# A new order of the same steps, and 113 copies on the other engine, in a one-core attention and MLP kernel

## Chip, core and metric

One core of one Trainium2 chip runs the whole kernel. The metric is device time in microseconds (us); the kernel before takes 613.71 us, the median of three runs (613.70, 613.71, 615.13).

## What is computed

Attention with rotated queries and keys (batch 4, 8 heads, 576 tokens, 64 wide), then a two-layer MLP on its 2304 rows of 512, with 2048 hidden columns and a piecewise quadratic activation:

```python
q_rot, k_rot = rotate(q), rotate(k)
scores = np.matmul(q_rot, k_rot.transpose(0, 1, 3, 2)) / np.sqrt(D)
scores = scores - np.max(scores, axis=-1, keepdims=True)
attn = np.exp(scores)
attn = attn / (np.sum(attn, axis=-1, keepdims=True) + 1e-09)
x = np.matmul(attn, v).transpose(0, 2, 1, 3).reshape(B * S, H * D)
h = x @ w_in
g = np.where(h >= 1, h, np.where(h <= -1, 0.0, (h + 1) ** 2 / 4))
return g @ w_out
```

## The kernel before

**Numbers.** Products run on float16 pairs: a value is its rounded high part and the rest as low part, and a product is the sum of three matmuls (high by high, high by low, low by high). The high part is a plain scaled copy, which either ACT (line 314) or DVE (line 316) can make; the low part (line 324, or 545 in the softmax) is always DVE's. Batch 0 alone multiplies its scores in float32 (line 562), the others use pairs (line 564).

**Stages.** Weights come in eight chunks of w_in and w_out (`prep_w`, 1 MB loads at line 239). DVE joins their words in three steps (493, 495, 497), ACT makes the high part, PE subtracts it (430, 431) and ACT writes the low part (434). Queries and keys are rotated by DVE (`turn`, lines 287 to 295; the first k halves with PE's help, 305 and 306). v is squared for its scale (248), split into `vS`, and copied by DMA to the other partitions as `vM`. An item is one tile of 128 rows for one pair of heads: PE scores into `psS`, DVE takes the row maximum (534), ACT the exponential (536), DVE the reciprocal (541), then the high and low part go into `phl`, a DMA transpose (243) writes `pT`, and PE multiplies by v (612). `x_out` (623, 626) leaves the pair `xT`, the MLP's input. A step of the MLP is PE's first product into the one bank `psH` (720), ACT's copy `a` (737), the square `r` on DVE (732) or in two passes on ACT (734, 735), DVE's sum (740), the high part `g` on ACT (743) or DVE (746), the low part on DVE (748), and PE's second product (757). Finished rows are copied by ACT (770) and stored by SP.

**What sets the order.** The kernel first lists its 2180 steps in a `Plan`, each with its engine. `Plan.order` then takes them off that list by the numbers of `ORDER`: each number is the place, in what is left of the list, of the step that is written next. An engine runs its steps in the order in which they are written, one after the other; a step that waits holds all behind it on its engine. SP issues every load, store and transpose, so a transpose that waits for its `phl` holds the loads behind it. `Plan.pick` reads `ON_VECTOR`, one character for each high copy that may run on either engine (softmax, k, q, v, square, `g`; 328 in all): 1 is DVE, 0 is ACT.

```python
def pick(self, first="act", ahead=0):
    i = len(self.free)
    self.free.append(len(self.steps) + ahead)
    return ("dve" if ON_VECTOR[i] == "1" else "act") if i < len(ON_VECTOR) else first

def order(self):
    left = list(range(len(self.steps)))
    return [self.steps[left.pop(int(k))][3] for k in ORDER.split()]
```

Of the kernel before, what the change touches and what calls it, by code (L numbers as in the profile page):

```python
# [24 lines left out]
0 0 1 0 21 6 47 24 31 1 18 5 0 27 4 0 6 38 6 17 16 13 24 3 1 54 19 0 9 19 31 4 28 1 0 26 8 21 0 11 235 0 238 12  # L25
58 0 235 235 235 1 36 0 232 35 446 231 1 0 229 33 228 1 0 13 225 229 5 224 9 11 225 226 0 2 220 223 217 219 0 1
218 40 217 0 216 224 39 215 6 0 213 213 415 218 76 20 1 216 19 0 33 1 405 211 0 399 201 0 0 29 14 0 397 204 204
27 0 12 201 0 206 11 194 198 11 1 192 0 194 2 9 8 195 8 8 374 3 28 187 191 6 189 186 8 0 1 4 2 183 0 1 2 29 179 5
0 0 3 0 166 0 172 1 165 0 0 10 169 1 173 0 8 162 0 162 0 6 0 1 0 158 3 1 162 151 154 0 0 6 151 156 154 148 0 5
151 0 0 144 148 148 3 20 1 145 150 9 2 38 142 27 137 0 145 139 142 136 0 6 2 133 137 133 133 135 0 4 131 170 0  # L30
131 0 0 127 1 136 7 36 1 124 132 126 264 157 6 0 155 0 121 128 152 127 121 2 149 3 0 123 0 8 1 128 115 7 118 114
138 1 116 124 112 115 6 1 0 2 74 110 3 0 28 111 249 130 0 7 79 104 126 119 0 0 5 116 1 0 212 1 101 95 1 1 98 8 97
227 1 93 91 3 93 101 91 0 93 5 0 1 95 88 213 94 213 212 96 21 87 0 2 0 206 91 0 83 0 209 6 81 200 79 85 2 197 204
84 82 5 0 193 184 196 76 0 21 189 189 1 2 189 75 188 9 187 196 2 184 8 183 69 1 0 180 190 180 0 5 65 1 0 176 1 62
173 0 68 0 7 171 175 66 172 66 0 6 166 64 167 0 56 165 5 173 55 60 55 12 66 0 158 133 157 53 56 0 154 1 153 150
61 1 155 149 60 1 153 59 7 0 143 149 0 49 5 45 0 143 0 137 1 140 0 139 1 134 137 141 8 1 135 38 134 1 6 312 0 0 0
106 105 1 128 39 122 33 10 1 1 122 0 42 120 16 0 40 105 27 291 115 0 114 26 0 112 4 27 2 0 106 109 114 2 106 105
85 9 20 102 29 0 1 104 27 104 18 102 18 7 100 16 99 16 0 0 96 91 20 99 94 5 89 93 1 91 0 25 3 92 24 89 90 24 75
87 1 86 9 83 93 78 83 9 81 83 21 76 1 85 78 3 68 0 6 2 8 5 71 68 76 72 74 7 73 62 69 71 80 7 67 12 62 67 50 7 63
66 19 48 69 62 7 60 47 66 10 0 45 57 6 60 15 54 0 14 42 41 50 7 52 0 39 45 42 55 44 39 46 66 2 159 45 2 51 40 43  # L40
338 10 46 43 2 41 35 2 35 40 35 34 2 37 35 36 143 7 35 2 33 35 16 139 32 16 32 6 2 29 2 130 2 27 129 3 11 23 121
11 3 122 2 24 20 126 298 2 312 2 0 125 20 1 0 110 4 17 14 4 115 280 285 108 114 0 12 106 0 11 104 2 25 103 10 101
2 266 23 101 101 0 1 106 21 98 96 21 26 101 94 253 96 1 93 25 6 19 94 6 18 6 245 87 1 19 1 15 5 1 84 15 20 233 7
19 1 9 78 0 9 10 10 225 13 10 72 67 77 68 9 69 76 67 68 72 11 9 211 70 15 10 65 0 63 9 12 61 62 9 60 60 69 11 59
57 17 59 57 63 8 2 55 9 185 7 5 58 490 7 57 6 50 54 1 49 9 5 50 2 55 7 48 4 47 4 50 2 45 48 178 3 171 47 3 1 7 44
2 170 43 40 6 41 166 2 40 2 37 43 4 37 4 31 39 0 38 0 37 29 31 145 35 31 41 2 30 2 5 30 38 125 28 35 5 132 0 4 26
# [877 lines left out]
```

## Time and profile before

| | us | share of the span |
|---|---|---|
| median of three runs | 613.71 | |
| the profiled execution | 613.75 | |
| its span, first to last instruction | 612.0 | 100% |
| TensorE matmuls (PE) busy | 577.5 | 94% |
| TensorE weight loads (PEld) busy | 377.0 | 62% |
| VectorE (DVE) busy | 512.1 | 84% |
| ScalarE (ACT) busy | 414.8 | 68% |

The shares are averages over the whole span, and the engines' busy times overlap. Which engine others wait for differs from stretch to stretch, so the rows below are taken by stretch: busy time of each engine, then the gaps. In a row of an engine's timeline the bracket at the end gives the idle time ahead of the instruction and what ended it. Matmuls are pipelined, so the distance from one start to the next says more than the duration of one.

### The profile page before, as it was taken

Reading aid. Unit: us, or ns where it says so; the run is one execution under the profiler, and the core shown is the slowest. Engines: PE = TensorE matmul, PEld = TensorE weight load, DVE = VectorE, ACT = ScalarE, POOL = GpSimd, SP = SyncE. Lnnn points to the kernel's source line nnn. Section 1 sums busy time; section 2 is a strip of 40 time slices with the busy share of each in tenths; the row PEclk is TensorE's granted clock in tenths of the full one; section 3 lists DMA queues with packets and bytes.
Section 4 is the critical chain, followed back from the end, with each engine's and each line's share of the span. In section 5 each row is a group of like instructions: output and inputs, shape, how many; then the busy total and the mean of one; then the engine's idle time right before and its main releaser. Section 6 shows DMA issues by size and latency. Waiting matters only on the chain.

```text
span 612.0 us, 12593 instructions
## 1 busy us (share of the span) xinstructions
PE 577.5 (94%) x5074; PEld 377.0 (62%) x5074; DVE 512.1 (84%) x824; ACT 414.8 (68%) x844; POOL 0.7 (0%) x6
## 2 busy tenths in 40 slices
PE   4777998999999999999979999999999999999996
PEld 2434565666665767666657676666667666667673
DVE  5997998999999999999978899999878888824442
ACT  1886998999988888776867576857856474343121
POOL 0000000000000000000000000000000000000000
PEclk9868999999999999999999999999999999999999
DMA  8997999678968965897484756748544654700000
GB/s 298 329 305 173 325 307 253 173 176 148 240 159 171 241 148 94 143 149 205 82 229 94 140 107 113 136 79 140 120 78 91 95 123 91 122 19 17 2 36 17
DMA packets 182570, 91.32 MB, mean 149 GB/s; under 512 B 170608, under 2 KB 171888, under 8 KB 180464
## 3 DMA queue, kind: packets, MB, share of 16 engines
q1 hardware_dynamic: 182512, 90.52, 65.8%
q8 instruction: 39, 0.64, 0.4%
q14 instruction: 19, 0.16, 0.1%
HBM read 40.96 MB, written 4.72 MB: 75 GB/s over the span
## 4 chain that ended last, share of the span: by engine, by line
PE 55%; DVE 20%; ACT 10%; DMA 10%; issue 3%; SPq 1%; DVEq 0%; ACTq 0%
PE psH L720 20%; PE psO L757 20%; PE psV L612 6%; PE psS L564 4%; DVE phl L545 4%; DVE sca L534 4%; ACT p L536 3%; DMA pT<-phl 2%; ACT phl L314 2%; DVE r L740 2%; DVE g L748 2%; DMA dup<-in_km_dram 1%; PE psS L430 1%; PE psS L562 1%; DMA vM<-vS 1%
## 5 line engine op out<-in xcount | busy, mean ns | idle before, releaser
L720 PE MATMUL psH<-xT,w 128*128 128x256 f16 (+1 forms) x2112 | 206.8, 253 | 5.1 <-ACT a L737 5.0
L757 PE MATMUL psO<-w,g 128*128 128x512 f16 x864 | 203.3, 379 | 0.0
L720 PEld LDWEIGHTS <-w 128*128 128x128 f16 x2112 | 175.0, 98 | 38.9 <-issue 8.8
L536 ACT ACTIVATE p<-psS,sca 128x576 f32<-128x576 f32 x144 | 105.8, 737 | 49.3 <-DVE sca L534 31.0
L757 PEld LDWEIGHTS <-g 128*128 128x128 f16 x864 | 81.4, 98 | 83.8 <-issue 2.6
L545 DVE SCALAR_TENSOR_TENSOR phl<-p,sca,phl 128x576 f16<-128x576 f32 x144 | 115.9, 813 | 5.0 <-ACT phl L314 4.2
L534 DVE TENSOR_REDUCE sca<-psS 128x1 f32<-128x576 f32 x144 | 105.9, 751 | 10.0 <-PE psS L564 4.9
L314 ACT ACTIVATE phl<-p,sca 128x576 f16<-128x576 f32 x99 | 74.6, 767 | 19.1 <-DVE sca L541 10.7
L737 ACT ACTIVATE a<-psH 128x512 f32<-128x512 f32 x72 | 42.5, 590 | 62.3 <-PE psH L720 58.1
L740 DVE SCALAR_TENSOR_TENSOR r<-a,r 128x512 f32<-128x512 f32 x72 | 49.4, 687 | 19.9 <-ACT r L735 19.2
L748 DVE SCALAR_TENSOR_TENSOR g<-r,g 128x512 f16<-128x512 f32 x72 | 49.4, 686 | 7.6 <-ACT g L743 5.5
L564 PE MATMUL psS<-kT,qT 64*128 64x64 f16 (+1 forms) x576 | 44.9, 284 | 1.0 <-ACT p L536 1.0
L612 PE MATMUL psV<-pT,vS 128*64 128x320 f16 (+2 forms) x576 | 44.2, 277 | 1.0 <-DMA pT<-phl 1.0
L564 PEld LDWEIGHTS <-qT 64*128 64x128 f16 x576 | 22.5, 94 | 30.6 <-issue 13.8
L743 ACT ACTIVATE g<-r 128x512 f16<-128x512 f32 x41 | 25.6, 624 | 13.9 <-DVE r L740 7.1
L732 DVE SCALAR_TENSOR_TENSOR r<-a 128x512 f32<-128x512 f32 x28 | 19.3, 689 | 18.4 <-ACT a L737 18.0
L612 PEld LDWEIGHTS <-vS 128*64 128x64 f16 x576 | 28.0, 111 | 9.3 <-issue 5.7
L734 ACT ACTIVATE r<-a 128x512 f32<-128x512 f32 x44 | 27.4, 624 | 6.7 <-DVE g L748 6.1
L434 ACT ACTIVATE w<-psS,sca 128x341 f16<-128x341 f32 (+1 forms) x48 | 25.3, 539 | 7.8 <-PE psS L431 7.2
L612 PE MATMUL psV<-pT,vM 128*64 128x320 f16 (+2 forms) x360 | 26.0, 275 | 3.1 <-DMA vM<-vS 3.1
L735 ACT ACTIVATE r<-r 128x512 f32<-128x512 f32 x44 | 27.7, 630 | 1.4
L536 ACT ACTIVATION_READ_ACCUMULATOR p<-psS,sca 128x1 f32 x144 | 28.3, 196 | 0.0
(95 smaller groups left out, 522.9 us busy)
## 6 DMA issues: line engine op xcount, KB each, us to landing
w<-in_w_in_dram SPq DMA_DIRECT2D x7, 1024.0 KB, 6.4
w<-in_w_out_dram SPq DMA_DIRECT2D x6, 1024.0 KB, 8.0
rv<-in_vm_dram SPq DMA_DIRECT2D x8, 512.0 KB, 6.2
out_dram<-o SPq DMA_DIRECT2D x16, 256.0 KB, 2.4
rk<-in_km_dram SPq DMA_DIRECT2D x6, 576.0 KB, 5.4
dup<-in_km_dram SPq DMA_DIRECT2D x6, 576.0 KB, 4.5
rq<-in_qb_dram SPq DMA_DIRECT2D x4, 640.0 KB, 6.7
dup<-in_qb_dram SPq DMA_DIRECT2D x4, 640.0 KB, 4.0
```

The lines of the kernel that those rows point to most:

```text
L314: plan.add("act", act_cost(n), at, lambda: nc.scalar.activation(out=hi, in_=x, func=AF.Copy, scale=f), r=r, w=w)
L534: plan.add("dve", dve_cost(S, psum=True), at, lambda m=m, src=src: nc.vector.tensor_reduce(out=m, in_=src, op=ALU.max, axis=AX.X, negate=T ...
L536: plan.add("act", act_cost(S, psum=True, ptrs=2), at, lambda a=a, e=e, m=m, src=src: nc.scalar.activation(out=p32[e], in_=src, func=AF.Exp ...
L545: plan.add("dve", dve_cost(S, ptrs=1), at, lambda a=a, e=e, hi=hi, lo=lo: nc.vector.scalar_tensor_tensor(out=lo, in0=p32[e], scalar=rr[:, ...
L564: nc.tensor.matmul(out=psS[a][:, lo:hi], lhsT=qT[hf][d, l, j, c:c + 128], rhs=kT[ks][d, j, m, lo:hi], start=z == 0, stop=z == 2)
L612: nc.tensor.matmul(out=outs[a], lhsT=st, rhs=moving(a, blk), start=z == 0, stop=z == len(seq) - 1)
L720: nc.tensor.matmul(out=psH[:, n * i:n * i + n], lhsT=wi[ft // 2][:, wl, kk, 128 * (ft % 2):128 * (ft % 2) + 128], rhs=xfn(xl, kk), start=z ...
L735: nc.scalar.activation(out=r_s, in_=r_s, func=AF.Square, scale=-1.0, bias=1.0)
L737: plan.add("act", act_cost(512, psum=True, ptrs=0), at, lambda one=one: nc.scalar.activation(out=a, in_=psH, func=AF.Relu, scale=2.0 ** -7 ...
L740: plan.add("dve", dve_cost(512), at, lambda one=one: nc.vector.scalar_tensor_tensor(out=r, in0=a, scalar=one, in1=r, op0=ALU.max, op1=ALU. ...
L748: plan.add("dve", dve_cost(512), at, lambda g=g, one=one: nc.vector.scalar_tensor_tensor(out=g[:, 1], in0=r, scalar=-one, in1=g[:, 0], op0 ...
L757: nc.tensor.matmul(out=psO[pos[tt]], lhsT=g[:, gl, n * i + 128 * tt:n * i + 128 * tt + 128], rhs=wo[ft // 2][:, wl, ft % 2, :], start=ft = ...
```

## The change

Only the two tables differ: the numbers of `ORDER`, and `ON_VECTOR`. The steps, what each computes and what each needs are the same. In `ON_VECTOR` 113 of the 328 characters differ: 50 copies go from ACT to DVE and 63 from DVE to ACT. Of the softmax's 576-wide copies 21 go to DVE and 28 to ACT, of the squares 9 and 14, of the `g` copies 16 and 18, of those of k, q and v 4 and 3. A copy of either table's first lines:

```diff
 ORDER = """
-0 0 1 0 21 6 47 24 31 1 18 5 0 27 4 0 6 38 6 17 16 13 24 3 1 54 19 0 9 19 31 4 28 1 0 26 8 21 0 11 235 0 238 12
+1 30 0 0 0 26 73 6 6 11 0 9 33 22 15 0 19 0 13 1 0 59 78 20 58 37 1 0 0 16 53 0 19 1 0 23 48 243 0 47 16 26 0 238
...
 ON_VECTOR = (
-    "00000000000000000000000000000000000000000000000000010000000000000000000000000000100100100011000000000000"
+    "00100000000000000000000000000000000000000000000000000100000000000010000000000000000000000000000000100000"
...
```

What the numbers do is seen in the order of the instructions. First SP, from the program's start: `in_km` are halves of keys, `in_qa` of queries, `in_rot` is the table `rt` of cosines and sines, `in_w_in` and `in_w_out` are chunks of the weights (`w` is the tile that also holds the second halves of the first keys and queries). Before:

```order
L239 DMA rt<-in_rot_dram 128x1152
L239 DMA w<-in_km_dram 128x576
L239 DMA rk<-in_km_dram 128x576
L239 DMA w<-in_qa_dram 128x256
L239 DMA rq_85<-in_qa_dram 128x256
L239 DMA w<-in_qa_dram 128x256
L239 DMA rk<-in_km_dram 128x576
L239 DMA rq_85<-in_qa_dram 128x256 x2
L239 DMA w<-in_qa_dram 128x256 x2
L239 DMA rk<-in_km_dram 128x576
L239 DMA w<-in_km_dram 128x576 x2
```

And in the changed kernel, from the same place:

```order
L239 DMA w<-in_km_dram 128x576
L239 DMA rt<-in_rot_dram 128x1152
L239 DMA rk<-in_km_dram 128x576
L239 DMA w<-in_km_dram 128x576
L239 DMA rk<-in_km_dram 128x576
L239 DMA w<-in_w_in_dram 128x2048
L239 DMA rq_85<-in_qa_dram 128x256
L239 DMA w<-in_qa_dram 128x256
```

The first chunk of w_in has moved from behind the loads of all keys (it was the fifteenth load) to the sixth place, ahead of the first queries. DVE's order moves with it: behind four products of key halves (line 287) stand 493 and 495 on this chunk, where 493 stood behind the second maximum before.

On PE, at the first product by v (`pT_74`, `vS` into `psV`), some 45 us into the trace of before. Lines with + stand here now; the same scores (562) and two pieces of a weight chunk's low part (430, 431) stood behind that whole product before:

```order
+L562 MATMUL psS_92<-kT_62,qT_64 128x512
+L562 MATMUL psS_93<-kT_62,qT_64 128x512
+L562 MATMUL psS_92<-kT_62,qT_64 128x64
+L562 MATMUL psS_93<-kT_62,qT_64 128x64
+L430 MATMUL psS_93<-o,kT_63 128x341
+L431 LDWEIGHTS kT_63
+L431 MATMUL psS_93<-w,kT_63 128x341
+L430 MATMUL psS_92<-o,kT_63 128x341
+L431 LDWEIGHTS kT_63
+L431 MATMUL psS_92<-w,kT_63 128x341
 L612 LDWEIGHTS vS
 L612 MATMUL psV<-pT_74,vS 64x128
```

One score item and two weight pieces have moved ahead of the product by v.

On SP, some 90 us into the trace, the loads of one chunk of both weights between transposes of softmax items. Before:

```order
L243 DMA_TRANSPOSE pT_74<-phl_72 128x18x128
L239 DMA w<-in_w_in_dram 128x2048
L243 DMA_TRANSPOSE pT_75<-phl_73 128x18x128
L239 DMA rq_85<-in_qa_dram 128x1024
L239 DMA w<-in_w_out_dram 128x2048
```

And now:

```order
L243 DMA_TRANSPOSE pT_74<-phl_72 128x18x128
L239 DMA w<-in_w_in_dram 128x2048
L239 DMA w<-in_w_out_dram 128x2048
L243 DMA_TRANSPOSE pT_75<-phl_73 128x18x128
L239 DMA rq_85<-in_qa_dram 128x1024
```

The w_out load has moved ahead of a transpose and a load.

On ACT, some 310 us into the trace, where batch 3's v is squared (line 248, from `rv`). Before:

```order
L536 ACTIVATE p_1_70,sca<-psS_93,sca 128x576
L248 ACTIVATE dup_87,sca<-rv 128x1024
L539 ACTIVATE sca<-sca 128x2
L743 ACTIVATE g_81<-r 128x512
L737 ACTIVATE a<-psH 128x512
L314 ACTIVATE phl_73<-p_0_69,sca 128x576
L248 ACTIVATE dup_87,sca<-rv 128x1024
```

And now the two squares, with what stands ahead of them:

```order
L314 ACTIVATE phl_72<-p_0_69,sca 128x576
L314 ACTIVATE phl_72<-p_2_71,sca 128x576
L743 ACTIVATE g_80<-r 128x512
L536 ACTIVATE p_1_70,sca<-psS_92,sca 128x576
L536 ACTIVATE p_2_71,sca<-psS_93,sca 128x576
L737 ACTIVATE a<-psH 128x512
L248 ACTIVATE dup_87,sca<-rv 128x1024
L539 ACTIVATE sca<-sca 128x2
L248 ACTIVATE dup_87,sca<-rv 128x1024
```

The squares have moved back by two softmax items, some twelve steps of ACT, and stand together; the two `rv` loads have moved on SP behind one transpose more.

## Rows read from the trace of the kernel before

**Rows 1.** Windows by stage: busy us and instructions per engine, granted clock, DMA.

```profile
0.00:60.00 60.00, 40.24 (x185) 22.89 (x185) 46.79 (x86) 36.24 (x76) 0.70 (x6) 0.83 0.92 277
60.00:200.00 140.00, 134.69 (x1233) 85.85 (x1230) 134.60 (x193) 128.82 (x254) 0.00 (x0) 1.00 0.89 216
200.00:300.00 100.00, 99.99 (x929) 66.68 (x927) 97.21 (x157) 80.18 (x167) 0.00 (x0) 1.00 0.79 160
300.00:345.00 45.00, 41.08 (x371) 27.36 (x369) 36.19 (x63) 31.32 (x64) 0.00 (x0) 1.00 0.66 147
345.00:600.00 255.00, 254.23 (x2338) 171.09 (x2336) 195.20 (x326) 136.81 (x286) 0.00 (x0) 1.00 0.45 84
```

**Rows 2.** Chain of waits, two pieces of it: start us, us, what.

```profile
191.38 1.42 PE psH L720 x12
...
196.68 1.31 PE psH L720 x12
```

**Rows 3.** DVE's timeline, 0 to 20 us: start, us, what, idle before.

```profile
6.33 0.76 DVE L287 TENSOR_TENSOR w<-w,rt 128x576 f32<-128x576 f32 x1 [4.98 <-DMA w<-in_km_dram]
...
8.95 0.76 DVE L287 TENSOR_TENSOR rk<-rk,rt 128x576 f32<-128x576 f32 x1 [0.33 <-DMA rk<-in_km_dram]
...
12.13 1.47 DVE L287 TENSOR_TENSOR w<-w,rt 128x576 f32<-128x576 f32 x2 [1.00 <-DMA w<-in_km_dram]
...
16.70 0.69 DVE L493 TENSOR_SCALAR xT<-w 128x1024 uint32<-128x1024 uint32 x1
```

**Rows 4.** DVE's timeline, 40 to 58 us.

```profile
46.06 0.69 DVE L493 TENSOR_SCALAR xT<-w 128x1024 uint32<-128x1024 uint32 x1 [1.32 <-DMA w<-in_w_in_dram]
...
53.61 0.76 DVE L534 TENSOR_REDUCE sca<-psS 128x1 f32<-128x576 f32 x1 [3.54 <-PE psS L431]
```

**Rows 5.** PE's timeline, 39 to 56 us.

```profile
39.08 1.50 PE L430 MATMUL psS<-xT,kT 128*128 128x341 f32 x2 [2.70 <-DVE sca L534]
...
48.44 0.75 PE L612 MATMUL psV<-pT,vM 128*64 128x128 f16 x10 [3.15 <-DMA vM<-vS]
...
49.65 2.29 PE L562 MATMUL psS<-kT,qT 64*128 64x512 f32 x8
51.86 0.84 PE L430 MATMUL psS<-o,kT 128*128 128x341 f32 x2
```

**Rows 6.** DVE's timeline, two waits between 94 and 186 us.

```profile
102.80 0.69 DVE L493 TENSOR_SCALAR o<-w 128x1024 uint32<-128x1024 uint32 x1 [1.84 <-DMA w<-in_w_out_dram]
...
169.15 1.36 DVE L287 TENSOR_TENSOR rk<-rk,rt 128x1152 f32<-128x1152 f32 x1 [1.94 <-DMA rk<-in_km_dram]
```

**Rows 7.** Chain of waits at 96 us.

```profile
96.11 6.59 DMA w<-in_w_out_dram
```

**Rows 8.** Table of waits: engine, line, releaser: us in total, times, longest.

```profile
ACT dup L248 <- DMA rv<-in_vm_dram: 4.5, 2, 2.4
```

**Rows 9.** PE's timeline, 304 to 330 us, its two gaps.

```profile
315.22 2.78 PE L720 MATMUL psH<-xT,w 128*128 128x256 f16 x24 [1.69 <-ACT a L737]
...
320.92 1.47 PE L720 MATMUL psH<-xT,w 128*128 128x256 f16 x12 [1.63 <-ACT a L737]
```

**Rows 10.** Groups by line and shape: busy us, mean ns of one, idle before.

```profile
L314 ACT ACTIVATE phl<-p,sca 128x576 f16<-128x576 f32 x99 | 74.6, 767 | 19.1 <-DVE sca L541 10.7 <-DMA pT<-phl 4.9 <-DVE sca L272 2.6
...
L734 ACT ACTIVATE r<-a 128x512 f32<-128x512 f32 x44 | 27.4, 624 | 6.7 <-DVE g L748 6.1 <-DVE sca L541 0.2
...
L316 DVE TENSOR_SCALAR phl<-p,sca 128x576 f16<-128x576 f32 x45 | 23.1, 517 | 2.8 <-DMA pT<-phl 2.0
...
L732 DVE SCALAR_TENSOR_TENSOR r<-a 128x512 f32<-128x512 f32 x28 | 19.3, 689 | 18.4 <-ACT a L737 18.0
```

**Rows 11.** Table of waits: ACT's high copies behind a transpose.

```profile
ACT phl L314 <- DMA pT<-phl: 4.9, 3, 3.1
```

**Rows 12.** Windows around the first product by v.

```profile
40.00:48.00 8.00, 5.18 (x19) 2.33 (x16) 6.62 (x14) 4.86 (x10) 0.00 (x0) 0.50 0.99 288
```

**Rows 13.** Table of waits of SP's queue: stores of outputs.

```profile
SPq L239 <- ACT o L770: 77.3, 6, 40.8
```

More of the change, by code (lines that the diff above doesn't have):

```diff
@@ L89 @@
 ON_VECTOR = (
-    "00000000000000000000000000000000000000000000000000010000000000000000000000000000100100100011000000000000"
-    "00101000001010100100000000001011010000000010110001000000110001001001100110110100010101010100001110101100"
-    "10001011011011100111110110001000011100110111100001000000011110010011111011011010011110001001111000110100"
-    "1111111011110110"
+    "00100000000000000000000000000000000000000000000000000100000000000010000000000000000000000000000000100000"
+    "01010001011001010000001001000001000100011010100000110101101100011011110110000100100111001001100010101001"
+    "01000000110001010100000010000110011110010000100011100101010011010011001010110010100011001100101100001010"
+    "1101001100010111"
 )
```

108 rows, old and new, of the table ORDER are left out of this document.

## The prediction

> **What bounds the kernel now.** I read the stretches first, then the gaps of the engine that each stretch hangs on. The windows by stage [rows 1] give four regimes. From 200 to 300 us PE is busy 99.99 of 100 and from 345 to 600 us 254.23 of 255: TensorE is the bound there, and nothing that DVE or ACT do in those stretches can shorten them unless it makes PE wait. In 60 to 200 us PE has 134.69, DVE 134.60 and ACT 128.82 of 140: three engines almost full, so a wait of any of them is soon a wait of all, and PE is idle 5.3 us. In 0 to 60 us PE works 40.24 of 60, DVE 46.79, ACT 36.24: loads and the chain of first products set the pace, 19.8 us of PE are lost. In 300 to 345 us PE loses 3.9 of 45. So about 29 us in all are to be had by an order, most of them in the first minute of the trace, and what PE does when it is full stays: the number of matmuls is the same.
>
> That PE is really full where its busy share says so is seen in the spacing: twelve 256-column matmuls of the first MLP product follow each other in 1.31 us, 109 ns each [rows 2]. The Trainium skill ("Perfetto Trace Analysis", section "Identifying the Most-Contended Engine") says that matmul busy share does not tell how near the limit TensorE is, and to read the share of the weight loads instead. In 200 to 300 us that is 66.68 of 100 [rows 1], so by it TensorE would have a third of its time to spare there; the spacing of 109 ns without a gap speaks against that here.
>
> **The change part by part.** Steps, instructions and dependencies are the same; the order on each engine differs, and 113 of 328 high copies change their engine (50 from ACT to DVE, 63 the other way). I sum against the profiled execution, 613.75 us (span 612.0 and 1.75 outside it), which is 0.04 above the median of the three runs, 613.71.
>
> (A) The start, 0 to 60 us. What is lost there on DVE today: 4.98 us until the first rotation product, whose load landed at 6.33, then 0.33 and 1.00 on later loads [rows 3]; further on 1.32 us for the weight chunk at 46.06 and 3.54 us before the maximum at 53.61 [rows 4]. That last one comes from PE: the first P·V product waits 3.15 us for the copy into vM, and the next scores (2.29 us), on which the maximum hangs, stand behind it in PE's order [rows 5]. In the changed order those scores and two pieces of the weights' low part stand ahead of the P·V product, so PE has work during the wait and DVE gets its scores: 3.54 goes. The second w_in load moves on SP from behind the vM copies to ahead of the second transpose: 1.32 goes. Gain 4.86.
>
> Against it stands a slower first step. The first product now needs rt, w and rk: 576, 288 and 288 KB, 1152 where it was 864. The rate follows from the waits [rows 3] and the sizes, which are the shapes in SP's order at 4 bytes (128x576 is 288 KB, 128x256 is 128, 128x2048 is 1024): rt and the first w, 864 KB, had landed at 6.33, and at 12.13 all up to the first of the two w in a row, 2912 KB. That is 353 KB/us. 288 KB more are 0.8 us. Behind four such products DVE now has the first step on the w_in chunk (L493), whose load is sixth on SP: 2752 KB with those ahead of it, landing at 6.33 + 1888 / 353 = 11.7 us. The four products, 0.68 us from one to the next, end at 7.1 + 2.7 = 9.8, so it waits 1.85. The start costs 4.98 + 0.8 + 1.85 = 7.6 us of waiting instead of 6.3, 1.3 more. Net A = -4.86 + 1.3 = -3.5 us. DVE is the engine to sum on, since the weight words that it does early (today from 16.70 on, [rows 3]) no longer stand between the first softmaxes, though by the same arithmetic PE's first scores come some 3 us later. Bounds: -4.9 if the new waits hide, +2.0 if nothing of 4.86 is kept and the later first scores are paid with part of those 3 us.
>
> (B) 60 to 200 us. DVE waits 1.84 us at 102.80 for a w_out chunk and 1.94 at 169.15 for the next k half [rows 6]. The first load was issued only at 96.11, after a transpose that held SP, and took 6.59 [rows 7]. Now it stands directly behind the w_in load of the same chunk, ahead of that transpose, while its use keeps its place in DVE's work. The k half's load moves three places back, but its use goes from 149 to 165 us of DVE work. Both waits go: 3.8 us. Not all of it is time, because PE has only 5.3 us of idle in the stretch and the new order has waits of its own which I cannot see in advance; I take half, -2.0. Bounds 0 and -3.8.
>
> (C) 300 to 345 us. ACT waits twice for the rv load of the last batch, 4.5 us together, the longer one 2.4 [rows 8]; behind it in ACT's order stand the copies of the MLP's hidden block (L737), and PE's next products wait 1.69 us at 315.22 and 1.63 at 320.92 for two of them [rows 9], 3.3 us. In the changed order these squares stand behind two more softmaxes (about twelve ACT steps later). The load is also issued behind one transpose more, so a part of the wait may stay; of the 3.3 us I take 2.5. Bounds 0 and -3.3.
>
> (D) PE changes its tile shape (full, two rows, two columns) 181 times instead of 174. The same twelve matmuls take 1.42 behind a step of another shape and 1.31 behind their own [rows 2], 0.11 more: 7 x 0.11 = +0.7. Bounds 0 and +0.8.
>
> (E) The engine of the high copies. On balance 7 softmax highs and 5 squares more go to ACT. A softmax high is 0.767 on ACT and 0.517 on DVE, a square takes two passes of 0.624 there against one of 0.689 [rows 10]: ACT +5.4 + 6.2 = 11.6, DVE -3.6 - 3.4 = -7.0, smaller kinds aside. All but two or so of the moved ones lie behind 157 us, where ACT has cover: 80.18 of 100 in 200 to 300 [rows 1], while DVE, at 97.21, is relieved. I take 0; without that cover it would be up to 11.6 us over 400 us of trace.
>
> (F) New waits behind 200 us: today's 345 to 600 us lose 0.8 [rows 1]. Another order there can lose more, hardly less. I take +1.0, bounds 0 and +3.1, the longest wait for a transpose that the table of waits has [rows 11].
>
> Sum: -3.5 - 2.0 - 2.5 + 0.7 + 0 + 1.0 = -6.3; 613.75 - 6.3 = 607.5 us.
>
> **The rivals.** (1) The front comes too late. If w_in, now early on SP, lands as late as its words are made today (from 16.70, [rows 3]) the DVE chain stands at the start and A gives nothing or costs its upper bound: 613.75 - 2.0 - 2.5 + 0.7 + 1.0 = 611.0 up to 613.0. For it: the load is 1 MB, and 128 KB loads for the first scores stand behind it. Against: every wait so far was released in issue order at the same rate. Chance 0.17.
>
> (2) All waits go and the clock is up sooner. From 40 to 48 us the granted clock averages 0.50 (1.2 of 2.4 GHz) with PE busy 5.18 of 8 [rows 12]; the same weight piece takes 1.50 us at 39.08 and 0.84 at 51.86 [rows 5]. If PE, no longer held at P·V, gets the full clock some six pieces sooner, at 0.66 each 4 us, of which perhaps 3 lie on the path, and no new waits come: 613.75 - 3.5 - 3.0 - 2.0 - 2.5 + 0.7 = 603.4. Against: P·V and scores of the start still wait for loads. Chance 0.10.
>
> (3) Slower: transposes late. SP is one queue; a transpose waits there behind whatever stands ahead of it, among it the stores of outputs, for which the queue waited six times, 77.3 us together [rows 13], at places where that did no harm. The change moves stores ahead of transposes at some three places (one in batch 1, two in batch 2). A transpose that comes late holds ACT's next high copy and PE's P·V, and PE's products behind it, by up to 3.1 us [rows 11]. Each such place in the part where PE is full costs 3.1: with two the gain is gone (613.6), from three it is slower, 607.5 + 9.3 = 616.8. Against: stores wait for ACT's copy at the end of a block, and transposes stand at many places with a softmax of slack. Chance 0.13.
>
> (4) DVE, not PE, sets the pace after 200 us, so that the -7.0 of E come off: 600.5. The rows speak against it (PE 99.99 of 100). Chance 0.02. The rule of the Trainium skill named above would lead here.
>
> **How the numbers follow.** Forecast 0.58, rivals 0.17, 0.10, 0.13 and 0.02. Two kernels of this kind can be told apart from 0.3% on, 1.84 us: faster is under 611.9, slower over 615.6. Faster: 0.56 of the forecast, 0.09 of rival 1, rivals 2 and 4, in sum 0.77; slower 0.12 from rival 3; the rest, 0.11, is the same. The forecast's own spread is 604 to 611. The range goes from 602.5 (rival 2, less a little) to 613.0 (rival 1's upper end); it leaves out rival 3, rival 4 and the tail of rival 2, under 0.2.
>
> **What would show it.** A right: P·V still waits for vM near 45 us but DVE's 3.54 is gone, the first DVE product begins near 7.1, the wait for w_in is under 2 us, and the stretch 0 to 60 holds 2 to 4 us more PE work. B right: no DVE wait over 0.5 us for w_out or rk; PE over 136.5 of the 140. C right: ACT's L248 waits under 1 us and PE's waits for L737 make under 2 us in all. D and E right: the PE-full stretches keep 99.7% and more. Wrong would be: w_in landing after 13 us; PE's idle in 60 to 200 us unchanged or more; PE waiting for transposes at P·V behind 200 us.

## The result, and the profile after

The changed kernel takes 607.25 us, the median of 4 runs (604.95 to 608.31), against 614.42 for the kernel before (four runs, 613.70 to 615.22): 0.988 of the time, 95% interval 0.9845 to 0.9911. The forecast was 607.5. As a difference, 7.2 us were measured where 6.3 were forecast: a fourth run of the kernel before moved its median from 613.71 to 614.42. The profiled execution took 607.59 us, span 605.7 against 612.0. The time was right to a quarter of a microsecond, and most of the sum's terms were not; the runs below show which.

The page of the kernel after, its first two parts and the shares of the chain that ended last:

```profile
span 605.7 us, 12611 instructions
...
PE 578.2 (95%) x5074; PEld 376.2 (62%) x5074; DVE 505.0 (83%) x811; ACT 426.1 (70%) x862; POOL 0.7 (0%) x6
...
PE 82%; DVE 8%; ACT 4%; DMA 3%; issue 1%; SPq 1%; DVEq 0%; ACTq 0%
```

PE's busy time has hardly moved (577.5 before), so the 6.3 us of span come out of PE's idle time, 34.5 us before and 27.5 after. Where it went is seen in the windows by stage of the kernel after (columns as in [rows 1], whose 60 to 200 us is here three lines):

```profile
0.00:60.00 60.00, 43.21 (x213) 24.43 (x215) 49.16 (x89) 37.70 (x79) 0.70 (x6) 0.94 0.98 285
60.00:110.00 50.00, 44.43 (x434) 27.71 (x430) 45.65 (x61) 42.88 (x86) 0.00 (x0) 0.93 1.00 286
110.00:165.00 55.00, 54.67 (x505) 35.35 (x503) 54.66 (x82) 53.26 (x107) 0.00 (x0) 1.00 0.83 176
165.00:200.00 35.00, 34.96 (x307) 23.21 (x306) 34.90 (x54) 33.09 (x66) 0.00 (x0) 1.00 0.78 182
200.00:300.00 100.00, 99.89 (x907) 64.89 (x906) 96.66 (x157) 82.91 (x172) 0.00 (x0) 1.00 0.70 146
300.00:345.00 45.00, 45.00 (x421) 30.44 (x419) 41.30 (x70) 29.47 (x62) 0.00 (x0) 1.00 0.78 179
345.00:600.00 255.00, 254.96 (x2302) 169.91 (x2300) 182.66 (x304) 146.07 (x297) 0.00 (x0) 1.00 0.43 82
```

And the same windows of the kernel before, where [rows 1] has only their sum:

```profile
60.00:110.00 50.00, 46.73 (x476) 30.42 (x473) 47.54 (x64) 45.18 (x89) 0.00 (x0) 1.00 1.03 289
110.00:165.00 55.00, 54.32 (x501) 34.13 (x498) 54.59 (x80) 53.26 (x107) 0.00 (x0) 1.00 0.85 180
165.00:200.00 35.00, 33.64 (x262) 21.30 (x260) 32.48 (x51) 30.37 (x60) 0.00 (x0) 1.00 0.77 170
```

PE's idle time changed by -3.0 us in 0 to 60, by +2.3 in 60 to 110, -0.35 in 110 to 165, -1.3 in 165 to 200, +0.1 in 200 to 300, -3.9 in 300 to 345 and -0.7 in 345 to 600. How much of such a number is chance shows in the run with the squares moved (below), whose order is that of before up to 310 us: its PE is busy for 38.75, 46.66, 53.89, 34.19 and 99.51 us in the five stretches up to 300, up to 1.5 away from the kernel before. From 110 us to the end of work PE now has next to no gap. One stretch got worse, 60 to 110 us, and it took most of what the first minute had gained.

DVE's timeline of the kernel after, its waits in the first 100 us:

```profile
6.19 0.76 DVE L287 TENSOR_TENSOR rk<-rk,rt 128x576 f32<-128x576 f32 x1 [4.85 <-DMA rk<-in_km_dram]
...
10.61 0.69 DVE L493 TENSOR_SCALAR xT<-w 128x1024 uint32<-128x1024 uint32 x1 [1.66 <-DMA w<-in_w_in_dram]
...
49.37 1.56 DVE L534 TENSOR_REDUCE sca<-psS 128x1 f32<-128x576 f32 x2 [0.76 <-ACT w L434]
...
51.78 0.69 DVE L493 TENSOR_SCALAR o<-w 128x1024 uint32<-128x1024 uint32 x1 [0.85 <-DMA w<-in_w_out_dram]
...
82.34 0.70 DVE L493 TENSOR_SCALAR xT<-w 128x1024 uint32<-128x1024 uint32 x1 [2.31 <-DMA w<-in_w_in_dram]
...
93.52 0.76 DVE L534 TENSOR_REDUCE sca<-psS 128x1 f32<-128x576 f32 x1 [1.37 <-PE psS L587]
```

The 3.54 before the maximum [rows 4] is 0.76, and the waits of 1.84 and 1.94 [rows 6] are gone. A new one of 2.31 us stands at 82.34, for the load of the fifth w_in chunk. It reaches PE, whose timeline there reads:

```profile
84.39 1.50 PE L720 MATMUL psH<-xT,w 128*128 128x128 f16 x24
87.95 0.84 PE L430 MATMUL psS<-xT,kT 128*128 128x341 f32 x2 [2.06 <-DVE sca L534]
...
89.48 1.50 PE L430 MATMUL psS<-xT,kT 128*128 128x341 f32 x2 [0.43 <-ACT p L536]
```

The two L430 rows are the same piece of a weight chunk: 0.84 us at one clock, 1.50 at the other. The granted clock of the kernel after around it (PEclk is the third number from the end; 0.5 is 1.2 GHz, 1.00 is 2.4):

```profile
84.00:88.00 4.00, 1.94 (x28) 1.52 (x26) 4.00 (x7) 3.41 (x6) 0.00 (x0) 1.00 1.09 366
88.00:92.00 4.00, 3.57 (x10) 1.31 (x14) 4.00 (x6) 3.75 (x9) 0.00 (x0) 0.59 1.03 308
92.00:96.00 4.00, 4.00 (x24) 1.79 (x17) 2.27 (x5) 1.90 (x6) 0.00 (x0) 0.56 1.01 298
96.00:100.00 4.00, 3.36 (x16) 1.59 (x14) 4.00 (x5) 4.00 (x8) 0.00 (x0) 1.00 1.02 299
```

After 2.06 us without work PE ran 8 us near the lower level. In the kernel before the clock is 1.00 throughout 60 to 110.

**PE's work against time.** Busy time grows when the clock falls, so the stretches are compared in another way too: each PE step is given the time it takes in a run of its own kind (563.2 us in all), and the table, worked out from the timelines, has the time by which a kernel reached the same amount of work, less that of before. A single execution is good to 1 or 2 us here: kernels with the same order up to 60 us differ there by up to 2.

| work done, us | 30 | 60 | 160 | 280 | 360 | 560 |
|---|---|---|---|---|---|---|
| reached by before at | 59.8 | 92.1 | 197.8 | 321.7 | 403.5 | 604.0 |
| after | -4.3 | +3.3 | -1.3 | -5.1 | -6.7 | -6.9 |

The kernel after is 4.3 us ahead at 60 us, 3.3 behind at 92, and wins its time between 92 and 400. The experiments ask three things: whether the new wait at 82 us took the front's gain (they show that it took part of it at most), what of the front lasts, and what the second half is worth by itself.

### The profile page after: what moved, and what is told of

Its sections match the earlier page's. It is cut to its first block, busy times and chain, and to the rows that moved or that the text cites. A ratio compares the mean times of both kernels' runs of the same rounds, so it can differ in the third digit from the quotient of the medians.

```text
span 605.7 us, 12611 instructions
## 1 busy us (share of the span) xinstructions
PE 578.2 (95%) x5074; PEld 376.2 (62%) x5074; DVE 505.0 (83%) x811; ACT 426.1 (70%) x862; POOL 0.7 (0%) x6
## 4 chain that ended last, share of the span: by engine, by line
PE 82%; DVE 8%; ACT 4%; DMA 3%; issue 1%; SPq 1%; DVEq 0%; ACTq 0%
PE psH L720 30%; PE psO L757 30%; PE psV L612 8%; PE psS L564 7%; DMA w<-in_w_in_dram 2%; PE psS L430 2%; PE psS L562 2%; DVE sca L534 1%; DVE phl L545 1%; DMA w<-in_w_out_dram 1%; ACT p L536 1%; PE psS L590 1%; DVE xT L495 1%; ACT w L314 1%; ACT phl L314 1%
## 5 line engine op out<-in xcount | busy, mean ns | idle before, releaser
L536 ACT ACTIVATE p<-psS,sca 128x576 f32<-128x576 f32 x144 | 105.8, 736 | 41.5 <-DVE sca L534 33.2
L314 ACT ACTIVATE phl<-p,sca 128x576 f16<-128x576 f32 x106 | 79.1, 767 | 19.4 <-DVE sca L541 19.3
L612 PE MATMUL psV<-pT,vS 128*64 128x320 f16 (+2 forms) x576 | 43.7, 275 | 0.9 <-DMA pT<-phl 0.9
L743 ACT ACTIVATE g<-r 128x512 f16<-128x512 f32 x43 | 26.9, 625 | 18.1 <-DVE r L740 15.3
L734 ACT ACTIVATE r<-a 128x512 f32<-128x512 f32 x49 | 30.7, 626 | 4.3 <-DVE g L748 3.5
L612 PEld LDWEIGHTS <-vS 128*64 128x64 f16 x576 | 27.5, 109 | 9.7 <-issue 6.8
L735 ACT ACTIVATE r<-r 128x512 f32<-128x512 f32 x49 | 30.9, 630 | 1.6
L430 PE MATMUL psS<-xT,kT 128*128 128x341 f32 (+1 forms) x48 | 21.1, 526 | 5.2 <-DVE sca L534 2.1
```

Source lines behind the costliest of these rows:

```text
L314: plan.add("act", act_cost(n), at, lambda: nc.scalar.activation(out=hi, in_=x, func=AF.Copy, scale=f), r=r, w=w)
L430: nc.tensor.matmul(out=bank, lhsT=idn, rhs=y[:, cut], start=True, stop=False)
L536: plan.add("act", act_cost(S, psum=True, ptrs=2), at, lambda a=a, e=e, m=m, src=src: nc.scalar.activation(out=p32[e], in_=src, func=AF.Exp ...
L612: nc.tensor.matmul(out=outs[a], lhsT=st, rhs=moving(a, blk), start=z == 0, stop=z == len(seq) - 1)
```

## The experiments

All times are medians, each with its ratio to the kernel before in the same call and the 95% interval.

**The new wait, taken out.** The kernel after with one load moved on SP: the w_in load that DVE waits for at 82.34 changes places with one that is needed 50 us later.

```diff
 L243 DMA_TRANSPOSE pT_74<-phl_72 128x18x128
+L239 DMA w<-in_w_in_dram 128x2048
+L243 DMA_TRANSPOSE pT_75<-phl_73 128x18x128
 L239 DMA kT_63<-in_w_in_dram 128x2048
-L243 DMA_TRANSPOSE pT_75<-phl_73 128x18x128
-L239 DMA w<-in_w_in_dram 128x2048
```

> The changed kernel with two loads exchanged on SP: the w_in load of the fifth chunk (issued at 76.23 us there, landed at 82.24, DVE waits 2.31 us for it at 82.34) trades places with the w_in load of the last chunk, which lies ready for 50 us before its use. Theory: that wait is what made the stretch 60 to 200 us lose what the two old waits gave back; behind it PE is idle 2.06 us at 87.95 and its granted clock is 0.56 to 0.59 from 88 to 96 us. With the wait gone PE keeps its clock and the kernel takes 4 us less than the changed one: 603 to 604 us, 0.984 of the kernel before. Rival: DVE, ACT and PE are all nearly full there, and another wait takes its place: 606 to 607.5 us, 0.988 to 0.990.

605.77 us, 0.9869 (0.9844 to 0.9894), below the rival's range and over 1.7 us above the theory's. The wait is gone and the clock stays at 1.00 from 80 to 100 us, yet the stretch gains only part of it (windows of this kernel):

```profile
60.00:110.00 50.00, 45.85 (x459) 29.28 (x460) 47.58 (x63) 44.08 (x87) 0.00 (x0) 0.97 1.07 294
```

45.85 against 44.43, and new waits of 0.93 and 0.88 us on DVE at 64.94 and 95.77. The time can't be told apart from the 0.988 of after. So the new wait was not what the front's gain went into, or something of nearly the same length stood right behind it.

**All loads of the first 200 us by need.** The kernel after with seven loads on SP in the order in which their waits ended, of which the first piece:

```diff
 L239 DMA rk<-in_km_dram 128x1152
-L239 DMA w<-in_w_in_dram 128x2048
+L239 DMA w<-in_w_out_dram 128x2048
 L239 DMA dup_88<-in_qb_dram 128x1280
...
 L239 DMA vM<-vS 64x2048 x2
-L239 DMA w<-in_w_out_dram 128x2048 x2
+L239 DMA w<-in_w_in_dram 128x2048
+L239 DMA w<-in_w_out_dram 128x2048
```

> The changed kernel with seven loads in another order on SP: chunk 2's w_out ahead of chunk 3's w_in, and the fifth chunk's two loads and the sixth chunk's w_in ahead of those two of the last chunks that lie ready for 37 and 50 us. Nothing else differs. Theory: DVE's waits for weight loads (0.85 at 51.78, 2.31 at 82.34, and 0.88 that came at 95.77 when only the 2.31 was taken away) all go, and it takes 3 to 4 us less than the changed kernel: 603.5 to 604.5 us. Rival: between 60 and 110 us the loads are not what binds, as taking the 2.31 us away gave 1.5 us: 605 to 607 us.

607.32 us, 0.9881 (0.9852 to 0.9909): nothing gained, as the rival had it. From 11.3 to 200 us no DVE wait on a load is left that is longer than 0.1 us, the clock is 1.00, and PE still loses 6.4 us of the 50 (windows of this kernel):

```profile
60.00:110.00 50.00, 43.57 (x448) 27.24 (x447) 47.17 (x62) 43.23 (x86) 0.00 (x0) 1.00 1.08 293
```

PE's waits there are many and short, for ACT's low parts (`w`, 434) and for transposes, 0.2 to 1.45 us each. Waits for weight loads are not what holds 60 to 110.

**One step of A by itself: the scores ahead of the product by v.** The kernel before with only those four rows moved on PE.

```diff
 L431 MATMUL psS_92<-w,kT_63 128x342
+L562 MATMUL psS_92<-kT_62,qT_64 128x512
+L562 MATMUL psS_93<-kT_62,qT_64 128x512
+L562 MATMUL psS_92<-kT_62,qT_64 128x64
+L562 MATMUL psS_93<-kT_62,qT_64 128x64
 L612 LDWEIGHTS vS
...
-L562 MATMUL psS_92<-kT_62,qT_64 128x512
-L562 MATMUL psS_93<-kT_62,qT_64 128x512
-L562 MATMUL psS_92<-kT_62,qT_64 128x64
-L562 MATMUL psS_93<-kT_62,qT_64 128x64
 L430 MATMUL psS_92<-o,kT_63 128x341
```

> The kernel before with one step moved on PE: the first product by v stands behind the next scores, not ahead of them; nothing else differs. Theory (part A): the 3.54 us that DVE waited at 53.61 come from that order, so they go, and the kernel takes 2.5 to 4 us less: 609.5 to 611 us. Rival: the gain of the start comes from the weight words that DVE does early, and the order on PE gives little: 613 us or more.

613.08 us, 0.9976 (0.9957 to 0.9995). 1.5 us gained by the ratio where 2.5 to 4 were expected, so the rival's time came. DVE's wait, which the prediction blamed on those scores, is still there. DVE's timeline of this kernel:

```profile
52.73 0.76 DVE L534 TENSOR_REDUCE sca<-psS 128x1 f32<-128x576 f32 x1 [3.17 <-PE psS L431]
```

And PE's:

```profile
44.26 2.40 PE L562 MATMUL psS<-kT,qT 64*128 64x512 f32 x8 [0.64 <-ACT w L434]
...
48.39 0.74 PE L612 MATMUL psV<-pT,vM 128*64 128x128 f16 x10 [1.17 <-DMA vM<-vS]
...
51.18 1.34 PE L430 MATMUL psS<-o,kT 128*128 128x341 f32 x2
52.32 0.37 PE L431 MATMUL psS<-w,kT 128*128 128x341 f16 x1
```

The scores are done at 46.66. The maximum starts at 52.73, after the weight piece of 51.18 and 52.32, which PE writes into the same tile `psS` beside them. The releaser that the row names, line 431, is that piece, which still stood behind the product by v. The kernel keeps both in one tile: scores in columns 0 to 575 of `psS`, the weight pieces from 576 on. In this trace and in that of the kernel before, none of the eight score matmuls updates a semaphore, while line 431 does, and the maximum waits for that semaphore: the wait stands in the program.

**The two weight pieces as well.** The kernel before with scores and both pieces ahead of the product by v, as the kernel after has it.

```diff
 L431 MATMUL psS_92<-w,kT_63 128x342
-L612 LDWEIGHTS vS
-L612 MATMUL psV<-pT_74,vS 64x128
...
 L562 MATMUL psS_92<-kT_62,qT_64 128x512
...
 L431 MATMUL psS_93<-w,kT_63 128x341
+L612 LDWEIGHTS vS
+L612 MATMUL psV<-pT_74,vS 64x128
...
```

> The kernel before with the first product by v moved on PE behind the next scores and behind two weight pieces, as in the changed kernel; nothing else differs. Moving it behind the scores alone left DVE's wait at 3.17 us, and it ended with the second piece, not with the scores (they were done 6 us earlier). Theory: the maximum waits for the piece, which writes into the same tile psS; with the pieces ahead of the product by v too, DVE's wait falls under 1 us and the kernel takes 3 us less than before: 610.5 to 611.5 us. Rival: the wait was never on the path, since DVE has weight words to make up anyway: 612.5 us or more, like the run with the scores alone (613.08).

615.44 us, 1.0008 (0.9990 to 1.0025). The mechanism is confirmed and the gain is not. DVE's timeline of this kernel:

```profile
51.41 0.76 DVE L534 TENSOR_REDUCE sca<-psS 128x1 f32<-128x576 f32 x1 [0.24 <-PE psS L431]
...
80.16 1.36 DVE L287 TENSOR_TENSOR dup<-dup,rt 128x1152 f32<-128x1152 f32 x1 [1.26 <-DMA dup<-in_km_dram]
...
87.51 1.42 DVE L534 TENSOR_REDUCE sca<-psS 128x1 f32<-128x576 f32 x2 [1.73 <-PE psS L431]
...
96.11 0.82 DVE L545 SCALAR_TENSOR_TENSOR phl<-p,sca,phl 128x576 f16<-128x576 f32 x1 [1.03 <-ACT phl L314]
...
105.65 0.69 DVE L493 TENSOR_SCALAR o<-w 128x1024 uint32<-128x1024 uint32 x1 [1.81 <-DMA w<-in_w_out_dram]
```

3.17 has become 0.24. Ahead by 1.5 us at 60 us (by the table at the end of this section), the kernel is 2.2 behind at 92: waits of 1.26, 1.73 and 1.03 have come where the kernel before has none, and the 1.81 at 105.65 is the old 1.84 [rows 6].

**The product put back.** The kernel after, with the product by v ahead of those scores and pieces again, as before.

```diff
 L431 MATMUL psS_92<-w,kT_63 128x342
+L612 LDWEIGHTS vS
+L612 MATMUL psV<-pT_74,vS 64x128
...
```

> The changed kernel with the first product by v put back on PE ahead of those scores and two pieces; nothing else differs. Theory: PE waits some 3 to 5 us for the copy into vM, the maximum behind it waits too, and 2.5 to 4 us of the gain go: 609.5 to 611 us. Rival: the early weight words carry the gain of the start, and the order on PE is worth under 1 us: 607 to 608.3 us.

609.52 us, 0.9920 (0.9894 to 0.9946): by the ratios some 2.6 us of the gain are lost (0.9920 against 0.9878, of 614), though the two intervals still overlap. DVE's timeline of this kernel has a wait of 6 us in its place:

```profile
53.43 0.82 DVE L545 SCALAR_TENSOR_TENSOR phl<-p,sca,phl 128x576 f16<-128x576 f32 x1 [6.01 <-ACT phl L314]
```

**The front alone.** The order of the kernel after up to 53 us, then that of before.

```diff
-ORDER: the steps up to 53 us as in before
+ORDER: the steps up to 53 us as in after (some 200 of 2180)
 ORDER: the last 1980 steps as in before
```

> The first 53 us of the changed kernel's order on all engines, then the kernel before's order and engines (one w_out load and one k load trade places at the seam). Theory: the front is worth about 4 us by itself and its gain is kept, since the new wait of the changed kernel at 82 us is not in it: 609 to 610.5 us. Rival: what the front gains is given back where DVE, ACT and PE are all full, 60 to 110 us: 612.5 us or more.

613.40 us, 0.9969 (0.9944 to 0.9994). By 60 us it is 3.0 ahead, at 92 us 2.1 behind, and it ends 1.9 us faster by the ratio: hardly more than the four rows alone (0.9976). In its profiled execution the gain ends in one wait of PE, for the transpose of a softmax item:

```profile
61.23 0.64 PE L612 MATMUL psV<-pT,vS 128*64 128x128 f16 x8 [2.99 <-DMA pT<-phl]
```

That transpose lands at 61.19 here, at 60.01 in the kernel before, where PE comes to its product at 60.14 and does not wait, and at 59.67 in the kernel after: its time did not follow PE's gain. Behind the wait the granted clock is 0.52 and 0.62 over two stretches of 4 us, which costs PE some more.

**Both halves apart.** In these kernels and the next each part brings its engines along; only 4 of the 113 copies that change theirs lie ahead of 165 us. The steps between the two counts in a cut are those that one order had done at the seam and the other had not; they stand in the second part's order. First the new half to 165 us, then the order of before:

```diff
-ORDER: the steps up to 165 us as in before
+ORDER: the first 671 steps as in after
 ORDER: the last 1463 steps as in before
```

> The complement: the changed kernel up to 165 us (671 steps), the kernel before behind it. Theory (all of the gain is made behind 165 us): 613.5 to 615.5 us, like the kernel before. Rival (the front's gain reaches the end): 609.5 to 612 us.

615.47 us, 1.0009 (0.9988 to 1.0029), as expected. The whole first half of the change gains nothing here. Windows of this kernel:

```profile
0.00:60.00 60.00, 44.33 (x229) 24.58 (x231) 49.55 (x90) 38.20 (x81) 0.70 (x6) 0.89 0.97 286
60.00:110.00 50.00, 43.43 (x424) 26.97 (x419) 45.46 (x60) 42.71 (x85) 0.00 (x0) 0.97 1.04 286
```

Four us more in the first minute (40.24 before), 3.3 less in the next 50. It also keeps the second wait of [rows 6], which the order of the second half sets: 3.18 us for `rk` at 171.20.

The old half to 165 us, then the order of after:

```diff
 ORDER: the first 672 steps as in before
-ORDER: the steps behind 165 us as in before
+ORDER: the last 1433 steps as in after
```

> The kernel before up to 165 us (672 of 2180 steps, with their engines), the changed kernel's order and engines behind it. In the profiles the front's gain of the changed kernel (4.3 us at 60 us) is gone at 92 us, and at 165 us, by PE's work done, it stands 0.7 us behind the kernel before. Theory: nothing of the first 165 us reaches the end, and all of the gain is made behind them, 1.7 us at 165 to 177 and about 5.5 between 290 and 370: 606.5 to 608.5 us with the old first part, as with the new one. Rival: the front's gain reaches the end as work that DVE has done ahead, and what PE lacked at 165 us was only the order: 609.5 to 611 us.

610.28 us, 0.9920 (0.9899 to 0.9942). 4.9 us come from the second half alone, although the seam has waits of its own (0.87 on DVE at 172.99, 1.50 on PE at 169.64). The time is the rival's, 609.5 to 611, not the theory's.

The same with the four rows of scores moved as in the third experiment:

```diff
 L431 MATMUL psS_92<-w,kT_63 128x342
+L562 MATMUL psS_92<-kT_62,qT_64 128x512
...
 L612 LDWEIGHTS vS
```

> The old first part and the new second part, and in the first the one step moved on PE that gave 0.9976 by itself (the first product by v behind the next scores). Theory: small gains of the two halves add, since behind 165 us no wait is left that could take it back: 605 to 606.5 us, a little faster than the changed kernel. Rival: as the wait of DVE there stayed at 3.17 us, those 1.5 us were spread, not gain: 606.5 to 608.5 us.

608.52 us, 0.9887 (0.9863 to 0.9910), at the rival's upper end. By the medians the move is worth 1.8 us here (the intervals overlap by 0.0011), and with it the old first half stands level with the kernel after (0.9878).

**The old front, with the new order from 80 us.** The order of before to 80 us with the four rows moved, then that of after.

```diff
 ORDER: the steps up to 80 us as in before
+ORDER: the four L562 rows ahead of the product by v
-ORDER: the steps behind 80 us as in before
+ORDER: the last 1683 steps as in after
```

> The kernel before up to 80 us (302 steps, the fifth chunk's w_in load early on SP, as it was) with the first product by v behind the next scores, and the changed kernel's order and engines behind that. It differs from the run with the old first half and the same moved step (608.52) only in whose order holds 80 to 165 us. Theory: the changed order takes away the waits at 102.80 and 169.15 (3.8 us) wherever it starts from, and its own new wait at 82 us comes from the order before 80, which is not in this kernel: 605 to 606.5 us. Rival: 80 to 165 us is bound by DVE's work, 54.6 of 55 us behind 110, and waits taken away there only move PE's: 607.5 to 609 us, like that run.

606.90 us, 0.9867 (0.9839 to 0.9894), between the theory's time and the rival's. At most those four rows of the new front are needed for the time of the kernel after. Windows of this kernel:

```profile
60.00:110.00 50.00, 45.74 (x454) 28.87 (x449) 47.68 (x63) 45.18 (x90) 0.00 (x0) 0.97 1.06 298
110.00:165.00 55.00, 54.68 (x496) 34.90 (x493) 54.67 (x81) 53.35 (x107) 0.00 (x0) 1.00 0.85 174
165.00:200.00 35.00, 35.00 (x310) 23.63 (x308) 34.91 (x55) 33.03 (x66) 0.00 (x0) 1.00 0.79 183
```

It gains its time from 110 us on, as the kernel after does. This kernel and the one with the w_in load moved have the lowest ratios of all, 0.987, and neither can be told from the kernel after.

**Term C by itself.** The kernel before with the two squares of batch 3's v next to the third, behind two softmaxes on ACT.

```diff
-L248 ACTIVATE dup_87,sca<-rv 128x1024
 L539 ACTIVATE sca<-sca 128x2
...
-L248 ACTIVATE dup_87,sca<-rv 128x1024
 L536 ACTIVATE p_2_71,sca<-psS_92,sca 128x576
...
+L248 ACTIVATE dup_87,sca<-rv 128x1024 x2
 L248 ACTIVATE dup_87,sca<-rvL 64x512
```

> The kernel before with two steps moved on ACT: the two squares of the last batch's v stand behind two more softmax items (together with the third, small one); nothing else differs, the loads not either. Theory (part C): ACT's waits of 2.44 and 2.02 us and PE's gaps of 1.69 and 1.63 go, the kernel takes 3 to 4 us less: 610 to 611 us. Rival: the steps that hang on the squares (scale, split of v, copies to vM) come late, and PE waits at the next product by v instead: 612.5 us or more.

613.10 us, 0.9979 (0.9963 to 0.9995): 1.3 us by the ratio where 3 to 4 were expected, so the rival's time came here too, though not its wait: PE waits for no product by v in this stretch. The windows of this kernel show the stretch itself gain 2.9 us of PE (41.08 before):

```profile
300.00:345.00 45.00, 43.98 (x410) 29.61 (x408) 38.36 (x66) 33.59 (x67) 0.00 (x0) 1.00 0.76 152
```

This profiled execution took 611.40 us, 2.35 less than that of before, while the median of twelve is 613.10; how much of the 2.9 is chance, one execution does not tell. ACT's wait for a transpose behind the stretch (2.67 us at 338.14, line 314) is no price of the move: the kernel before has it too, 3.06 at 340.38.

**The engines of the copies.** The kernel after with the `ON_VECTOR` of before.

```diff
 ON_VECTOR = (
-    "00100000000000000000000000000000000000000000000000000100000000000010000000000000000000000000000000100000"
+    "00000000000000000000000000000000000000000000000000010000000000000000000000000000100100100011000000000000"
...
```

> The changed kernel's order, with each high copy on the engine on which the kernel before had it (113 copies go back). Theory (part E): behind 200 us PE sets the pace and the engine of a copy costs nothing: 606.5 to 608.5 us, like the changed kernel. Rival: the order was made for these engines, and ACT and DVE queue up where the copies go back; PE gets gaps of some us: 610 us or more.

631.60 us, 1.0287 (1.0257 to 1.0317): 2.9% slower than before and 4.1% slower than after, where no change against after was expected. Windows of this kernel:

```profile
200.00:300.00 100.00, 93.97 (x848) 61.57 (x845) 90.31 (x147) 72.39 (x152) 0.00 (x0) 1.00 0.70 143
...
345.00:600.00 255.00, 248.20 (x2220) 164.66 (x2217) 195.32 (x329) 138.12 (x289) 0.00 (x0) 1.00 0.46 88
```

And its table of waits (total us, times, longest):

```profile
ACT p L536 <- DVE sca L534: 52.4, 41, 3.7
...
PE psS L564 <- ACT p L536: 7.6, 16, 1.2
...
PE psH L720 <- ACT a L737: 4.9, 9, 1.2
```

In the stretches where PE was full it now loses 6.0 of 100 and 6.8 of 255. ACT waits for DVE's maxima for 52.4 us in all (33.2 in the kernel after), and PE for ACT's exponentials and copies `a`, two rows that the kernel after has not in its table at all; the kernel before has them with 1.0 and 5.0 us. Over the whole span PE is idle 43.7 us (27.5 in the kernel after), and its records make it busy 586.1 us instead of 578.2, which no row explains. DVE and ACT do as much as in the kernel before, but in an order laid out for other steps on them.

The same table of work as above, for the kernels of the experiments:

| work done, us | 30 | 60 | 160 | 280 | 360 | 560 |
|---|---|---|---|---|---|---|
| after, the new wait out | -2.8 | +1.9 | -1.7 | -5.5 | -7.1 | -7.2 |
| after, loads by need | -2.2 | +1.7 | -0.9 | -4.8 | -6.4 | -6.5 |
| before, scores first | -0.9 | -0.9 | -2.8 | -2.4 | -2.3 | -2.3 |
| before, scores and pieces first | -1.5 | +2.2 | +2.0 | +2.0 | +2.0 | +2.0 |
| after, product back | +1.7 | +4.1 | +0.2 | -3.7 | -5.3 | -5.4 |
| new to 53 us, then before | -3.0 | +2.1 | -0.1 | -0.1 | -0.1 | +0.2 |
| new to 165 us, then before | -4.8 | +2.8 | +1.6 | +2.5 | +2.5 | +2.5 |
| old to 165 us, then after | +0.4 | +0.5 | +1.3 | -2.3 | -3.4 | -3.5 |
| the same, scores first | -1.3 | -1.0 | -0.3 | -4.0 | -5.6 | -5.7 |
| old to 80 us, scores first, then after | -0.7 | +2.7 | -1.7 | -5.5 | -7.2 | -7.3 |

The first two columns are some 60 and 92 us. The six kernels that are 1.5 to 4.8 us ahead in the first are 1.7 to 3.3 behind in the second, but two that aren't (the product back; old to 80 us) lose 2.4 and 3.4 as well: how much PE has done by 92 us does not follow how far it was at 60.

## Why the prediction was right, and where it was not

**The time was right by luck: two errors cancel.** The two halves measured apart show it. The prediction had -5.5 us for A and B together and -0.8 for C to F. The second half alone is worth -4.9 (0.9920); cut at 165 us, it has one of the two waits of B in it. The first half adds some 2.6 to it by the ratios (0.9920 to 0.9878 of 614), of which the seam's own waits may be a part, and nothing in front of the old second half (1.0009).

**(A), -3.5: right at 60 us, wrong at the end.** The kernel after is 4.3 us ahead there, inside the bounds, and DVE's 3.54 is gone. The step that failed is that a gain at 60 us would be one at 612. 60 to 110 us takes it back in every kernel whose front was clearly ahead; the new front alone ends at 0.9969, and the old front does as well as the new (0.9867 and 0.9878). Of A only the scores ahead of the product by v last: 1.5 us in the kernel before, 1.8 with the new second half, the first just clear of the noise and the second not; with the two pieces some 2.6 in the new order, and nothing (1.0008) in the old. Two details failed too. The 3.54 was put down to the scores, but it was the weight piece in the same tile `psS` (3.17 with the scores moved, 0.24 with the pieces moved as well); the row in [rows 4] names line 431, the piece, and was misread. And the slower first step wasn't there: the first product starts at 6.19, not 7.1, though 288 KB more had to land, and w_in was there at 10.61, not 11.7. The rate of 353 KB/us counts only the loads up to the one waited for. The windows show 205 GB/s from 0 to 6.33 us before and 229 from 0 to 6.19 after, some 1.3 and 1.4 MB, where 864 and 1152 KB were counted: later loads were already on the way beside them. (The first chunk of w_in was the sixteenth load before, not the fifteenth, with one load of keys behind it; the sum does not use this.)

**(B), -2.0: the waits went as said, the time came otherwise.** Both are gone, and 165 to 200 us gained 1.3 us of PE. But the move of loads that freed one chunk made the next late (2.31 at 82.34), PE stood still for 2.06 and lost clock, and the criterion "PE over 136.5 of 140" failed: 134.06. "Half of the waits is time" had no ground in a row. That removing the new wait, or all waits for loads, changes the end by less than the interval says the same: here waits on DVE were not lengths of time to be added up.

**(C), -2.5: too small.** PE has no gap at all in the stretch now, 45.00 of 45 where 41.08 stood: 3.9 us. The squares alone bring 2.9 of PE there and 1.3 at the end, so the term fits neither number. That the rest comes from the steps around them, which the new order has moved as well, is not shown by a run.

**(D), +0.7,** agrees with PE's busy time (577.5 to 578.2), but the clock changes that number too, so it isn't shown apart.

**(E), 0: the value fits, the reason was wrong.** With the new engines PE stays full (99.89 of 100 and 254.96 of 255). The old order with the new engines was not run, so the term by itself is not measured. The prediction said that ACT had cover and that the choice of engine costs nothing beside a full PE. With the old engines under the new order PE is not full, and the price is 24 us. The row that could have warned is [rows 1]: DVE at 97.21 of 100, where a copy more at a wrong place can delay a maximum.

**(F), +1.0: wrong sign.** The stretch from 345 to 600 us lost 0.8 us before and 0.04 now, a gain of 0.7 where +1.0 was taken as a price. By the windows C and F together brought 4.6 us, where the sum had 1.5, and A and B 2.4 (3.0 up to 60 us, less 0.6 from 60 to 200), where it had 5.5: 3.1 too much here, 3.1 too little there.

**The rivals.** Late transposes (3) did not come: the longest wait for one on PE is 0.88 us, at 79.80. DVE as the pace behind 200 us (4) is refuted: DVE has 12.5 us less work in 345 to 600 (195.20 to 182.66), and PE, full before, gained only its 0.7 of gaps; the 256-column matmuls of line 720 follow each other in 109 ns in both kernels. The rule of the Trainium skill that led there ("Perfetto Trace Analysis", section "Identifying the Most-Contended Engine") names the share of the weight loads as one of two measures, beside the arithmetic done against the peak, which was not worked out here. By weight loads, 169.91 of 255, a third of PE would still be free; the trace disagrees, since less work on DVE and the same spacing leave PE's time for its steps as it was. Of rival 2 the clock did come sooner in this execution, 0.94 over the first 60 us for 0.83; and in two kernels with the same order up to there 0.91 and 0.89, but the gain was given back like the rest. Rival 1 is refuted by w_in's 10.61.

**What stays open.** What takes the front's gain back between 60 and 110 us is not settled as one cause. PE's longest wait there is another one in most kernels: 2.06 us for a maximum in the kernel after, 2.99 for a transpose with the front alone, 1.94 for a transpose with scores and pieces first (at 82.06), 1.91 for a weight part of ACT with the old order to 80 us (at 83.12). Waits for weight loads and the clock are ruled out as the whole of it: without both PE still loses 6.4 of 50. DMA engines are busy at a share of 1.00 to 1.08 there in every kernel listed, so the transposes and copies of that stretch may be what can't come sooner; PE's short waits for ACT's weight parts speak for ACT's and DVE's own order as well. But the kernel before has a share of 1.03 there as well, and no run tells these apart.

## What to carry to other kernels

A gain in an early stretch counts only if the next stretch can keep it: build the hybrid that has the new order up to a point and the old one behind it, and the reverse, before adding up waits. Name the instruction that really releases a wait, among all that write the same tile, before moving another out of its way. An order and the choice of engines that it was searched with are one change; half of it can cost more than the whole gains, as the new order with the old engines did (24 us lost where the whole gained 7).

## What the runs showed of the hardware that was not expected

- A maximum over scores waited for a matmul into the same tile `psS`, in other columns: 3.17 us with the scores long done, 0.24 with that matmul moved too. The trace lays this to the program, not to the chip: line 431 updates the semaphore that the maximum waits for, and no score matmul does. What the chip would do without that wait, no run shows.
- One gap of 2.06 us on PE at 85.9 was followed by 8 us at a granted clock of 0.59 and 0.56; the same piece then took 1.50 us instead of 0.84. With the gap gone the clock stayed at 1.00 from 80 to 100 us. With the front alone, 2.99 us without work ahead of 61.23 were followed by a granted clock of 0.52 and 0.62 over the 8 us from 60 on, and the same piece took 1.50 us there too.
- 1152 KB had landed by 6.19 us where 864 KB had by 6.33: 288 KB more did not move the first wait. Several loads were on the way at once (205 GB/s up to 6.33 us are some 1.3 MB), so the bytes of the loads waited for don't set it alone.
